# Two heads change places in an attention and feed-forward kernel, and its written order of work is replaced

## The chip, the cores and the metric

The kernel runs on one core of one Trainium2 chip. The metric is the device time of one execution in microseconds (us); the time shown for the kernel before is the median of three runs. A profile is one execution seen by the hardware profiler; its "span" runs from the first to the last instruction of the program and is shorter than the device time.

The engines are named as the profile names them: PE is the matrix engine, PEld its weight loads, DVE the vector engine, ACT the scalar engine, POOL the general-purpose engine, SP the engine that only issues transfers (DMAs). "SPq" is SP's queue of instructions. A transfer that has arrived is said to have landed.

## The reference: what is computed

Four batches, eight heads, 768 positions, 64 numbers a head. Heads 0, 2 and 6 are "retrieval" heads: plain causal attention. The other five are "streaming" heads: a position sees the first four positions (the sink) and the last 64 (the window). The heads' outputs side by side are x (3072 rows of 512), and a feed-forward layer follows:

```python
scores = q @ k.T / sqrt(64)                    # per batch and head
keep   = causal if retrieval[h] else causal & (sink | last 64)
a      = softmax(where(keep, scores, -1e9))
x      = concat over heads (a @ v)             # 3072 x 512, float32
h      = x @ w_in                              # w_in 512 x 2048
out    = (h * sigmoid(beta * h)) @ w_out       # w_out 2048 x 512
```

## The kernel before, in words

**Units.** The work is cut into eight units: batch b and half u of the positions (384 queries each), n = 2b + u. Each unit goes through the same stages. Its q, k and v are loaded in float32 and cast to bfloat16; q and k are turned (units 0 to 2: by PE transposes of tile `c`, units 3 to 7: by DMA transposes `QK<-c`, called `turn_block`); PE makes the scores S(n, ...) into two-bank PSUM tiles `sp`; ACT takes the exponential into `es`; DVE multiplies masks in; PE adds up the exponentials (`sums` in units 0 and 1, `sums_d` later); PE multiplies with v (`pv`) into `sp` again; DVE multiplies by the reciprocal sums R (`norm`) into `xT`, four tiles of 128 x 384, each tile two heads of 64 rows. Then come 16 tiles `mm1` (w_in against `xT`, four matmuls into one PSUM bank `b`), for each a tanh on ACT (`swish_a`, output `t`) and a multiply on DVE (`swish_b`, output `gT`), and 48 matmuls `mm2` against w_out, copies (`osb`) and stores.

**The reciprocals' round trip.** In units 2 to 7 the sums go from PSUM to `sc`, by DMA to `rec` (`sums_turn`), through a DVE reciprocal, by DMA to a scratch in DRAM (`spread_w`, `rd<-rec`), and from there by DMA to all 64 rows of every head (`spread_r`, `R<-rd`; in odd units one small `q2f<-rd` more). `norm` needs it.

**Which heads share a tile.** `PAIRS` says which two heads are loaded, turned and scored together: (0, 2), (1, 3), (4, 5), (6, 7). `XT` says which two heads share a tile of `xT`: (1, 0), (2, 3), (4, 5), (6, 7). The rows of w_in must lie in the same order, so the rows of heads 1 and 0 are loaded swapped. `ORDER` and `QUARTERS` say where each head's sums lie; `spread_r` uses as many DMAs as it needs for rows at even distances in that order.

**Loading weights.** w_in and w_out come in four quarters of 1 MB each. A quarter of w_in (`load_w_in`) takes three DMAs, a quarter of w_out one. They land in a ring `wf` of three buffers, which v and the blocks of q and k (`load_block`) use too; POOL casts each in four parts (below: wi0 to wi15 and wo0 to wo15, four per quarter). A new load waits until an earlier buffer has been cast.

**The written order.** Every piece of work is a task, given to `add` with its engine, a price in us, what it needs, what it gives, and which ring buffers it takes. There are 1096. `SEQUENCE` is a list of their numbers and `CHOICE` a letter for each of 97 tasks that may run on one of several engines. `_Plan.run` walks the list and places each task as early as its engine and its needs allow:

```python
for o in (self.ops[i] for i in SEQUENCE):
    ...
    t = max([now[e]] + [done[n][0] - ... for n in needs])
    ...
    end = t + cost
    was, now[e] = now[e], end
    ...
    if dma:
        bus = max(bus, t + (0.5 if dma > 0.2 else cost)) + dma
        end = bus + (1.9 if dma > 0.2 else 3.2)
    order.append((t, i, f, e, t - was))
return [x[2:] for x in sorted(order, key=lambda x: x[:2])]
```

The tasks are emitted in order of their planned times, and every engine keeps that order (`_Ordered`). So on one engine the tasks follow each other as `SEQUENCE` has them, and a task that waits holds up all that follow on its engine. The prices decide only the planned times, not the length of anything on the chip. Line L112, which nearly every row of the profile names, is the helper that emits all instructions; rows are told apart by their tiles.

**Transfers share eight semaphores.** In the trace every DMA from the ninth on waits for the one eight before it to land. SP issues nearly all of them, in order, so a load that waits for a buffer also holds back the ones behind it.

**Start.** SP loads q, and ACT the first four k. PE runs filler matmuls in planned gaps of unit 0. A task `const_table` (an Exp of one column, on ACT) stands early in ACT's order.

Of the kernel before, what the change touches and what calls it, by code (L numbers as in the profile page):

```python
# [16 lines left out]
PAIRS = [(0, 2), (1, 3), (4, 5), (6, 7)]  # L17
XT = [(1, 0), (2, 3), (4, 5), (6, 7)]
# [10 lines left out]
QUARTERS = [[[1, 0], [2, 3], [4, 5], [6, 7]], [[2], [6], [0], [3, 5, 7, 1, 4]]]  # L29
# [3 lines left out]
ORDER = [[1, 0, 2, 3, 4, 5, 6, 7], [2, 6, 0, 3, 5, 7, 1, 4]]  # L33
# [4 lines left out]
    474, 475, 6, 466, 4, 8, 14, 468, 12, 478, 467, 20, 10, 0, 2, 16, 5, 469, 473, 9, 7, 33, 471, 29, 77, 34,  # L38
    31, 13, 89, 32, 15, 30, 37, 477, 18, 50, 38, 39, 51, 11, 79, 40, 85, 1, 56, 43, 52, 3, 490, 35, 25, 41,
    27, 36, 26, 57, 42, 28, 17, 44, 45, 21, 47, 78, 91, 48, 53, 80, 97, 54, 59, 86, 102, 480, 23, 100, 24,  # L40
    101, 58, 103, 60, 49, 116, 19, 46, 117, 118, 55, 61, 22, 120, 62, 463, 121, 485, 479, 492, 119, 122, 73,
    493, 90, 63, 92, 491, 123, 114, 75, 64, 74, 81, 115, 112, 76, 83, 125, 481, 65, 87, 126, 67, 113, 69, 484,
    66, 134, 482, 71, 68, 135, 483, 137, 108, 70, 500, 139, 109, 72, 488, 520, 82, 93, 524, 138, 84, 104, 464,
    140, 127, 489, 95, 465, 528, 521, 494, 105, 522, 529, 486, 532, 536, 495, 136, 525, 487, 530, 106, 142,
    526, 88, 533, 143, 534, 502, 540, 107, 98, 110, 503, 547, 505, 111, 94, 541, 128, 548, 131, 501, 542, 551,
    132, 124, 555, 141, 129, 96, 549, 556, 559, 133, 159, 130, 560, 504, 557, 99, 144, 552, 510, 499, 553,
    155, 145, 497, 537, 498, 538, 157, 156, 496, 146, 515, 507, 563, 158, 509, 561, 570, 508, 564, 160, 147,
    523, 571, 148, 506, 527, 565, 572, 163, 531, 167, 153, 149, 151, 511, 535, 171, 150, 512, 161, 152, 574,
    513, 165, 154, 578, 575, 514, 173, 582, 579, 576, 169, 580, 586, 583, 218, 518, 592, 584, 476, 587, 517,
    596, 588, 516, 470, 597, 519, 539, 593, 598, 162, 543, 546, 594, 168, 222, 550, 172, 554, 174, 170, 184,  # L50
    185, 558, 544, 164, 166, 562, 190, 186, 188, 191, 193, 175, 189, 566, 187, 600, 221, 196, 569, 573, 192,
    601, 577, 194, 581, 567, 219, 181, 602, 198, 220, 604, 199, 197, 182, 224, 608, 201, 200, 585, 609, 195,
    227, 225, 203, 605, 610, 589, 223, 204, 606, 228, 612, 202, 206, 590, 205, 619, 613, 207, 226, 176, 208,
    620, 177, 623, 621, 209, 591, 614, 210, 627, 631, 229, 628, 635, 632, 629, 237, 633, 636, 235, 642, 568,
    624, 637, 239, 646, 238, 650, 211, 647, 625, 240, 212, 178, 472, 269, 595, 651, 648, 241, 599, 652, 242,
    654, 179, 643, 249, 655, 603, 236, 252, 644, 213, 658, 250, 253, 607, 656, 659, 244, 660, 611, 247, 271,
    615, 245, 618, 622, 243, 251, 616, 254, 248, 273, 626, 180, 255, 630, 257, 183, 634, 246, 256, 638, 258,
    272, 641, 639, 259, 270, 617, 645, 260, 649, 261, 214, 216, 231, 215, 280, 653, 232, 657, 217, 275, 661,
    664, 662, 274, 278, 668, 665, 276, 672, 669, 666, 277, 676, 262, 673, 230, 233, 670, 674, 677, 279, 678,
    680, 684, 681, 691, 682, 263, 685, 695, 326, 692, 686, 699, 693, 696, 703, 700, 697, 707, 663, 701, 714,  # L60
    704, 708, 718, 289, 705, 709, 715, 722, 726, 716, 264, 723, 234, 667, 727, 290, 281, 671, 724, 293, 282,
    728, 675, 719, 283, 291, 730, 720, 679, 731, 292, 315, 284, 295, 732, 683, 296, 687, 298, 690, 694, 688,
    300, 297, 698, 319, 303, 294, 327, 301, 302, 702, 304, 328, 706, 265, 299, 329, 267, 266, 689, 305, 330,
    545, 268, 710, 306, 713, 717, 307, 721, 370, 725, 317, 736, 729, 737, 321, 740, 738, 316, 711, 733, 324,
    741, 744, 318, 734, 748, 320, 742, 745, 752, 322, 749, 746, 323, 756, 308, 753, 750, 763, 754, 325, 757,
    767, 764, 758, 771, 640, 765, 768, 775, 309, 772, 366, 769, 779, 773, 776, 786, 777, 790, 787, 286, 780,
    788, 334, 332, 285, 739, 335, 287, 794, 336, 781, 743, 795, 310, 337, 791, 796, 747, 338, 792, 798, 339,
    369, 802, 799, 346, 367, 803, 800, 751, 349, 373, 368, 804, 755, 347, 376, 759, 762, 288, 760, 341, 372,
    766, 344, 333, 375, 770, 340, 342, 371, 774, 343, 374, 351, 350, 345, 778, 354, 348, 377, 782, 352, 785,
    311, 353, 355, 313, 312, 356, 789, 357, 314, 793, 358, 386, 797, 331, 387, 735, 801, 390, 712, 412, 808,  # L70
    388, 812, 809, 378, 392, 813, 810, 805, 395, 379, 814, 816, 391, 783, 359, 380, 820, 806, 817, 360, 824,
    416, 821, 818, 828, 822, 825, 835, 393, 826, 839, 396, 829, 836, 397, 830, 843, 389, 837, 840, 847, 361,
    844, 841, 851, 394, 848, 845, 415, 858, 849, 862, 852, 413, 859, 866, 853, 414, 860, 870, 863, 417, 864,
    400, 811, 419, 871, 815, 398, 418, 872, 422, 819, 867, 823, 868, 421, 399, 874, 401, 381, 827, 875, 420,
    402, 876, 362, 403, 404, 364, 363, 761, 831, 834, 423, 365, 838, 842, 429, 846, 880, 832, 850, 405, 881,
    431, 406, 882, 884, 807, 432, 382, 383, 888, 885, 892, 889, 886, 384, 854, 424, 890, 893, 857, 433, 861,
    426, 833, 855, 865, 407, 894, 869, 385, 896, 900, 425, 897, 434, 898, 907, 436, 911, 901, 784, 908, 873,
    902, 856, 877, 909, 912, 915, 878, 913, 919, 430, 916, 879, 427, 923, 920, 917, 930, 924, 921, 934, 435,
    925, 938, 931, 942, 932, 939, 408, 943, 940, 410, 409, 935, 883, 887, 411, 946, 944, 443, 936, 947, 891,
    895, 446, 447, 948, 952, 444, 953, 438, 954, 899, 441, 903, 439, 956, 442, 445, 906, 957, 448, 437, 958,  # L80
    910, 449, 914, 451, 450, 440, 918, 904, 960, 452, 453, 922, 454, 961, 926, 455, 964, 962, 968, 965, 905,
    929, 969, 933, 966, 937, 970, 428, 941, 945, 927, 949, 456, 972, 928, 950, 457, 979, 973, 983, 980, 974,
    987, 981, 984, 991, 988, 985, 995, 989, 992, 1002, 996, 993, 458, 1006, 997, 1003, 1010, 1007, 1004, 1014,
    1008, 1018, 1015, 955, 1011, 1016, 1012, 1019, 951, 1020, 959, 963, 967, 971, 975, 978, 976, 982, 977,
    986, 990, 994, 998, 1001, 999, 1005, 459, 460, 1000, 461, 1009, 462, 1013, 1017, 1021, 1024, 1022, 1028,
    1025, 1023, 1032, 1029, 1026, 1036, 1030, 1033, 1040, 1037, 1034, 1044, 1038, 1041, 1051, 1045, 1042,
    1055, 1046, 1052, 1059, 1056, 1053, 1063, 1057, 1060, 1067, 1064, 1061, 1073, 1065, 1068, 1076, 1069,
    1079, 1077, 1027, 1080, 1078, 1031, 1081, 1074, 1082, 1075, 1085, 1083, 1035, 1086, 1084, 1039, 1087,
    1043, 1047, 1048, 1050, 1054, 1049, 1058, 1062, 1066, 1070, 1088, 1071, 1089, 1072, 1092, 1090, 1091,
    1093, 1094, 1095,  # L90
]
CHOICE = (
    "aaddagaggdgdadadadaadddaddaaddgaagggdaaadaadaaaddaaaddaggdgdgaggadggdgdaadaadaaadaadadadddadddaaa"
# [95 lines left out]
def kernel(  # L189
# [282 lines left out]
    def load_w_in(s):  # L472
        f = stg.tile([128, 2048], F32, name="wf", bufs=RINGS["wf"]).rearrange("p (a n) -> p a n", a=NP)

        def rows(r, n, tiles):
            return bass.AP(moe_w_in.tensor, moe_w_in.offset + r * d_ff + s * 2 * FS,
                           [[d_ff, n], [128 * d_ff, tiles], [1, 2 * FS]])
        sp.dma_start(out=f[:, 1:4, :], in_=rows(128, 128, 3))
        sp.dma_start(out=f[0:D, 0:1, :], in_=rows(D, D, 1))
        sp.dma_start(out=f[D:128, 0:1, :], in_=rows(0, D, 1))  # L480
        wst["i", s] = f
# [483 lines left out]
    def attention(n, early):  # L965
# [3 lines left out]
        for pi in range(NP if n < TD else 0):  # L969
            for nm in ("q2", "k2"):  # L970
                e = "act" if n == 0 and nm == "k2" else "sp"
                add(e, 0.47, lambda pi=pi, nm=nm, e=e: load_qk(x, pi, nm, ENG[e]), dma=0.63,
                    gives=[("f", n, pi, nm)], take=[(nm + "f", (n, pi), 1)])
                e = ("pool", "dve", "act") if early else ("pool",)
                add(e, [{"dve": 0.3, "pool": 0.47, "act": 0.41}[i] for i in e],
# [265 lines left out]
```

## Time and profile before

| what | value |
|---|---|
| device time, median of 3 runs | 242.45 us (241.02 to 242.52) |
| span of the profiled execution | 238.9 us |
| around the span, against the median | 3.55 us |
| PE busy | 224.3 us, 94% of the span |
| DVE, ACT, POOL busy | 153.9, 141.9, 90.8 us |
| mean granted clock of PE | 0.979 |
| moved by DMA | 43.14 MB |

How to read it: an engine's busy time is the union of its instructions. PE's matmuls overlap, so its busy time includes some slack that no row shows. "40 slices" cut the span in pieces of 6.0 us; a digit is a share in tenths. In a list of waits, "A <- B" means that A's engine stood idle until B had finished. The profiled execution's device time is not given; the span plus the 3.55 us stands for it.

### The profile page before, as it was taken

The page shows a single profiled execution, that of the slowest core. Times are in us where ns is not written, and L with a number is a line of the kernel's source. Part 1 is how long each engine was busy: PE and PEld are TensorE (multiplying, and loading weights), DVE is VectorE, ACT ScalarE, POOL GpSimd, SP SyncE. Part 2 cuts the span into 40 slices and gives each one's busy share as a digit, 9 for nine tenths or more (in the row PEclk, how much of TensorE's full clock was granted, in tenths as well). Part 3 has the DMA queues.
Part 4 walks back from the last instruction along what each step waited for, and adds up shares of the span by engine and source line. Part 5 has one row for each costly group of instructions (what it writes and reads, how often), then busy time and mean ns, then how long its engine had stood idle before and what let it go on. Part 6 is the DMA issues. An engine that isn't in the chain of part 4 may idle for free.

```text
span 238.9 us, 6057 instructions
## 1 busy us (share of the span) xinstructions
PE 224.3 (94%) x2359; PEld 128.6 (54%) x2385; DVE 153.9 (64%) x354; ACT 141.9 (59%) x238; POOL 90.8 (38%) x199
## 2 busy tenths in 40 slices
PE   8678996999999999999999999999999999999994
PEld 8535555555555456546544545564465555466553
DVE  4539869783968838865686548787475477157620
ACT  3858785456889518761679569707677437107611
POOL 7204759587632845696536173403600000000000
PEclk9956999999999999999999999999999999999999
DMA  6999699999989979999998999789910026211012
GB/s 197 273 307 321 205 258 354 300 314 211 175 196 240 211 162 189 214 230 223 225 231 179 169 230 231 149 178 216 219 71 3 0 92 150 80 44 47 0 44 88
DMA packets 92108, 43.14 MB, mean 181 GB/s; under 512 B 75936, under 2 KB 84848, under 8 KB 92080
## 3 DMA queue, kind: packets, MB, share of 16 engines
q1 hardware_dynamic: 90992, 41.98, 76.0%
q10 hardware_dynamic: 1088, 0.79, 1.1%
q8 instruction: 18, 0.29, 0.5%
q14 instruction: 10, 0.08, 0.1%
HBM read 32.38 MB, written 6.37 MB: 162 GB/s over the span
## 4 chain that ended last, share of the span: by engine, by line
PE 70%; DMA 9%; DVE 8%; SPq 4%; POOL 3%; ACT 3%; issue 2%; POOLq 0%
PE b L112 60%; PE sp L112 10%; SPq L112 4%; DMA QK<-c 3%; DMA wf<-in_v_dram 2%; POOL c L112 2%; DMA wf<-in_k_dram 2%; DMA q2f<-in_q_dram 2%; DVE es L112 2%; DVE gT L112 1%; ACT t L112 1%; DVE vs L112 1%; DVE QK L112 1%; ACT es L112 1%; DVE KP L112 1%
## 5 line engine op out<-in xcount | busy, mean ns | idle before, releaser
L112 ACT ACTIVATE t<-b,beta_h 128x384 f32<-128x384 f32 x128 | 72.4, 582 | 40.3 <-PE b L112 29.2
L112 DVE SCALAR_TENSOR_TENSOR gT<-t,b 128x384 bf16<-128x384 f32 x128 | 68.9, 551 | 37.1 <-ACT t L112 33.2
L112 PE MATMUL b<-xT,w_in 128*128 128x384 bf16 x512 | 90.3, 326 | 1.4 <-POOL w_in L112 0.9
L112 PE MATMUL b<-w_out,gT 128*128 128x512 bf16 (+1 forms) x374 | 87.1, 370 | 2.7 <-issue 1.8
L112 PEld LDWEIGHTS <-w_in 128*128 128x128 bf16 x512 | 49.0, 98 | 38.7 <-issue 2.6
L112 PEld LDWEIGHTS <-gT 128*128 128x128 bf16 x400 | 36.9, 98 | 38.7 <-issue 2.4
L112 ACT ACTIVATE es<-sp 128x768 bf16<-128x768 f32 (+3 forms) x64 | 49.1, 806 | 11.1 <-PE sp L112 10.7
L112 POOL CAST c<-wf 128x256 bf16<-128x256 f32 x60 | 23.2, 432 | 21.2 <-DMA wf<-in_q_dram 13.7
L112 PE MATMUL sp<-QK 64*64 64x64 bf16 (+6 forms) x402 | 19.9, 242 | 4.0 <-DVE QK L112 1.5
L112 ACT ACTIVATE osb<-b 128x512 f32<-128x512 f32 (+1 forms) x14 | 8.0, 568 | 23.9 <-PE b L112 16.9
L112 PEld LDWEIGHTS <-QK 64*64 64x64 bf16 (+1 forms) x402 | 10.4, 107 | 15.2 <-issue 12.1
L112 POOL COPY KP<-QK 128x64 bf16<-128x64 bf16 (+4 forms) x36 | 10.2, 332 | 21.6 <-DMA QK<-c 21.6
L112 POOL CAST w_in<-wf 128x512 bf16<-128x512 f32 x16 | 10.7, 699 | 15.2 <-DMA wf<-in_moe_w_in_dram 15.2
L112 POOL CAST vb<-wf 128x512 bf16<-128x512 f32 x18 | 12.2, 696 | 11.2 <-DMA wf<-in_v_dram 11.1
L112 DVE TENSOR_TENSOR es<-es,mask_c 128x256 bf16<-128x256 bf16 (+2 forms) x32 | 12.1, 394 | 4.2 <-ACT es L112 4.0
L112 DVE TENSOR_TENSOR es<-es,mask_s 128x800 bf16<-128x800 bf16 (+5 forms) x24 | 12.9, 551 | 2.7 <-ACT es L112 2.7
L112 DVE TENSOR_TENSOR xT<-sp,R 128x768 bf16<-128x768 f32 (+3 forms) x18 | 11.6, 687 | 4.0 <-PE sp L112 3.9
L112 DVE TENSOR_SCALAR osb<-b 128x512 f32<-128x512 f32 x11 | 7.5, 681 | 9.9 <-PE b L112 7.7
L112 PE MATMUL sp<-es,vb 128*64 128x64 bf16 (+3 forms) x243 | 13.8, 237 | 0.0
L112 POOL COPY vs<-vb 64x1536 bf16<-64x1536 bf16 (+2 forms) x9 | 12.2, 1361 | 2.5 <-issue 2.1
L112 PEld LDWEIGHTS <-vb 128*64 128x64 bf16 x243 | 11.8, 111 | 0.3
L112 POOL CAST w_out<-wf 128x512 bf16<-128x512 f32 x16 | 10.1, 667 | 2.2 <-DMA wf<-in_moe_w_out_dram 2.1
(91 smaller groups left out, 169.8 us busy)
## 6 DMA issues: line engine op xcount, KB each, us to landing
out_dram<-osb SPq DMA_DIRECT2D x23, 256.0 KB
wf<-in_v_dram SPq DMA_DIRECT2D x18, 256.0 KB
wf<-in_moe_w_out_dram SPq DMA_DIRECT2D x4, 1024.0 KB
wf<-in_q_dram SPq DMA_DIRECT2D x15, 256.0 KB
wf<-in_k_dram SPq DMA_DIRECT2D x15, 256.0 KB
R<-rd SPq DMA_DIRECT2D x9, 384.0 KB
wf<-in_moe_w_in_dram SPq DMA_DIRECT2D x4, 768.0 KB
q2f<-in_q_dram SPq DMA_DIRECT2D x12, 192.0 KB
```

Source lines behind the costliest of these rows:

```text
L112: ins = f(*a, **k)
```

## The change

One: `XT` becomes `PAIRS`, so tile 0 of `xT` holds heads 0 and 2, and tile 1 heads 1 and 3. `QUARTERS` and `ORDER` of even units follow: 0, 3, 1, 2 in place of 1, 0, 2, 3.

Two: `load_w_in` still issues three DMAs for a quarter: before, 768 KB on 128 partitions and twice 128 KB on 64; now 512 KB and twice 256 KB, all on 128 partitions.

Three: `spread_r`, whose code is the same, now needs three DMAs in place of two in units 2, 4 and 6, and four in place of three in 3, 5 and 7 (the small one not counted), because the heads' places are less even.

Four: prices of some tasks change, and `SEQUENCE` and `CHOICE` are new throughout.

```diff
-XT = [(1, 0), (2, 3), (4, 5), (6, 7)]
+XT = PAIRS
-QUARTERS = [[[1, 0], [2, 3], [4, 5], [6, 7]], [[2], [6], [0], [3, 5, 7, 1, 4]]]
+QUARTERS = [[[0, 3], [1, 2], [4, 5], [6, 7]], [[2], [6], [0], [3, 5, 7, 1, 4]]]
-ORDER = [[1, 0, 2, 3, 4, 5, 6, 7], [2, 6, 0, 3, 5, 7, 1, 4]]
+ORDER = [[0, 3, 1, 2, 4, 5, 6, 7], [2, 6, 0, 3, 5, 7, 1, 4]]
 SEQUENCE = [
-    474, 475, 6, 466, 4, 8, 14, 468, 12, 478, 467, 20, 10, 0, 2, 16, 5, 469, 473, 9, 7, 33, 471, 29, 77, 34,
+    474, 12, 14, 0, 8, 2, 475, 466, 479, 10, 6, 463, 469, 13, 478, 37, 15, 39, 4, 468, 473, 471, 477, 1, 25,
...
 def load_w_in(s):
-        sp.dma_start(out=f[:, 1:4, :], in_=rows(128, 128, 3))
-        sp.dma_start(out=f[0:D, 0:1, :], in_=rows(D, D, 1))
-        sp.dma_start(out=f[D:128, 0:1, :], in_=rows(0, D, 1))
+        sp.dma_start(out=f[:, 2:4, :], in_=bass.AP(moe_w_in.tensor, at + 4 * D * d_ff, [[d_ff, 128], [2 * D * d_ff, 2], cols]))
+        for t in range(2):
+            sp.dma_start(out=f[:, t, :], in_=bass.AP(moe_w_in.tensor, at + t * D * d_ff, [[2 * D * d_ff, 2], [d_ff, D], cols]))
...
-            add("sp", [1.33, 2.65][u], lambda: spread_r(x), ... dma=[6.2, 6.0][u],
+            add("sp", [2.0, 2.65][u], lambda: spread_r(x), ... dma=[3.8, 3.9][u],
...
-            add("sp", 1.3 if w == "i" else 0.65, ..., dma=3.5, ...)
+            add("sp", 1.6 if w == "i" else 0.5, ..., dma=3.1 if w == "i" else 2.9, ...)
```

The other prices that change: loads of q and k 0.63 to 0.65, blocks 3.5 to 3.65, v 3.5 to 3.6, `sums_turn` in odd units 1.5 to 1.7, `const_mask_new` 0.75 to 1.4.

What the new order says at the start, as the numbers of the tasks decode. Each engine's list, before and after:

```
SP before:  q of pairs 1 2 3, v2, q pair 0, v0 | unit 1: q0 q3, v1 (unit 0), k0 q2, wi4-7 (3 DMAs), k3, v2 (unit 1), wi0-3 (3), beta, wo0-3, q1 k1 k2, wi8-11, v0 v1, wo4-7, ...
SP after:   q of pairs 3 0 2, beta, q pair 1, v0 | unit 1: q0 q1 k0 q2 q3, v1 (unit 0), k2, v2 (unit 0), k3, wi0-3 (3 DMAs), k1, wi4-7 (3), wo0-3, wi8-11, v2 v1 v0, wo4-7, ...
ACT before: four loads of k, const_table among them; one cast; then copies and exponentials
ACT after:  four loads of k; two casts; then copies and exponentials; const_table is the 19th from the end
```

Ahead of `pv` of unit 1 PE has 10 tiles of `mm1` before and 12 after; ahead of the first `mm1` it has 14 groups of scores before and 16 after. The work on PE in total is the same list of tasks.

## Prediction

> **What bounds the kernel now.** I read the page first, then busy time in stretches of 10 us, then PE's waits, then the chain of waits and the timelines of the start.
>
> ```profile
> span 238.9 us, 6057 instructions
> ...
> PE 224.3 (94%) x2359; PEld 128.6 (54%) x2385; DVE 153.9 (64%) x354; ACT 141.9 (59%) x238; POOL 90.8 (38%) x199
> ...
> PEclk9956999999999999999999999999999999999999
> DMA  6999699999989979999998999789910026211012
> ```
>
> PE is the bound, at full clock but for the slices around 12 to 24 us; the transfers are about as full until some 170 us. The stretches show where PE has room:
>
> ```profile
> 0.00:10.00 10.00, 7.71 (x99) 6.99 (x99) 4.25 (x27) 5.50 (x11) 4.71 (x28) 1.00 0.89 227
> 10.00:20.00 10.00, 6.85 (x63) 3.64 (x63) 5.85 (x18) 6.58 (x11) 1.61 (x3) 0.61 1.13 307
> 20.00:30.00 10.00, 9.35 (x140) 6.19 (x139) 9.20 (x20) 8.18 (x13) 6.96 (x11) 0.88 0.80 249
> 30.00:40.00 10.00, 7.92 (x113) 4.61 (x115) 7.97 (x16) 7.57 (x14) 6.88 (x12) 1.00 1.09 297
> 40.00:50.00 10.00, 9.95 (x122) 6.13 (x113) 7.95 (x17) 4.61 (x8) 6.66 (x12) 1.00 1.01 321
> ```
>
> PE's busy time is the first figure after each length. It lacks 8.2 us before 40 us and hardly anything afterwards. From 40 us on PE waits for others only this much:
>
> ```profile
> PE b L112 <- issue: 1.8, 11, 0.2
> PE sp L112 <- DMA QK<-c: 0.5, 1, 0.5
> PE b L112 <- DVE gT L112: 0.2, 1, 0.2
> ```
>
> So a new order can win only in the first 40 us, and can lose anywhere. The start ends where PE last waits for data. That is `pv` of unit 1, which needs `vs`, a DVE copy:
>
> ```profile
> 39.08 1.51 DVE L112 COPY vs<-vb 64x1536 bf16<-64x1536 bf16 x2
> ```
>
> PE begins that `pv` at 40.66 and is full from there. One later place is as tight: the scores of unit 5 start right behind a chain of loads, casts and DMA transposes.
>
> ```profile
> 108.63 5.09 DMA wf<-in_k_dram
> ...
> 113.77 3.53 POOL c L112 x10
> ...
> 119.42 3.81 DMA QK<-c
> 123.27 0.50 PE sp L112 x4
> ```
>
> **Heads in pairs: PE and DVE.** In `pv` the first tile now pairs two retrieval heads and the second two streaming heads; before, one of each stood side by side. In the trace of `pv` of unit 2 the two halves of PE run side by side either way. The two mixed tiles took 0.573 us (85.411 to 85.984). Heads 4 and 5, both streaming, took 0.22 us for seven matmuls a side. One side's retrieval head took 0.187 + 0.109 + 0.056 = 0.35 us for its 384, 256 and 128 columns. New: 0.35 + 0.22 = 0.57 us. I take 0; bounds -0.05 and +0.1 us a unit. Sums, masks and `norm` keep counts and shapes.
>
> **Weights on 128 partitions.** In the quarter that landed around 19 us the 768 KB took 2.68 us (from the landing before it, by the trace's semaphore events), the halves 0.56 and 0.33. That is 0.89 us for 256 KB on 64 partitions, and 2.68 / 3 = 0.89 on 128. Three DMAs stay three, each about 0.5 us of SP. I take 0. Upper bound: as dear per MB as v, 1.15 us for 256 KB, so +1.0 us a quarter. Lower: as cheap as w_out, whose 1 MB landed 2.32 to 2.67 us after the landing before, so -0.9 to -1.2 us a quarter. Casts on POOL and the PE work ahead cover either, as the next part shows; with that cover gone the first quarter alone would move PE.
>
> **The start in the new order.** DMAs land one behind another: 0.65 us for q or k, 1.15 for v, 3.5 for w_in, 2.4 for w_out. Before, they landed with holes: q of pair 3 of unit 1 came 2.09 us after the last instead of 0.65, and with the waits for `wf` buffers there are about 4.7 us of holes up to 50 us. In the new order v2 no longer stands ahead of unit 0's last pair, and no load meets a buffer still in use. So I get unit 0's q and k by 8.4 us (before 9.43), the first two w_in quarters by 24.0 (before 24.9), the third by 30.0 (33.7), the last w_out by 45 (50.1). The first four casts of w_in end near 22.7 (before 27.3). Weights then wait for nobody in the first 40 us; before, one wait was 0.92 us.
>
> What remains is ACT and DVE. With casts of 0.45, copies 0.45, exponentials 0.75 and 0.2 us from engine to engine, ACT runs nearly without a hole from the first exponential at about 9.3 us to its last one before the first `swish_a`, which starts near 28.0; before it was 30.03. On DVE the spread constants (`sel`, 0.75) and a copy of `R` (0.96) leave the chain to the first `norm`. Then come masks, ten `swish_b` at 0.5, two casts of v and `vs` at 1.5, which ends near 38.8. So `pv` of unit 1 starts near 39.0 instead of 40.66, with 12 tiles of `mm1` done instead of 10. A tile is 0.65 us (eight matmuls in 1.47, less the last one's tail). Gain: 1.66 + 2 x 0.65 = 3.0 us. A hand count over some forty links may be off by 0.05 a link: bounds -5.0 (all holes filled) and +1.
>
> **The table load speaks against it.** `const_table` now stands near the end. Before, its load ran while ACT waited for data:
>
> ```profile
> 1.87 1.28 ACT L112 ACT_TABLE_LOAD   x1 [1.87 <-issue]
> ...
> 3.17 0.20 ACT L112 ACTIVATE warm<-warm 128x1 f32<-128x1 f32 x1
> 5.07 0.51 ACT L112 CAST c<-q2f 128x384 bf16<-128x384 f32 x1 [1.70 <-DMA q2f<-in_q_dram]
> ```
>
> It stands right ahead of the first ACTIVATE. In the new order the first is unit 0's first exponential; casts and copies are other operations in the trace. Behind it queue all of ACT's exponentials and copies, for which PE's two `sp` buffers wait. Cost between 0 (ahead of the casts again) and 1.28; I take +1.28, nearest to the row. The dummy itself, 0.20 us near the end, is hidden by ACT's waits for PE (29.2 us in all).
>
> The Trainium skill ("ScalarE: Activation LUTs", What ACT_TABLE_LOAD costs) gives about 1283 ns for the load plus about 1380 ns of drain, some 2.66 us a switch. The row agrees on 1.28 and shows no drain: ACTIVATE starts 0.02 us after the load. By the page the sum below would be 1.4 us worse, 242.2.
>
> **Reciprocals.** One more issue in `spread_r`, 0.6 us of SP. The bytes are the same, and the data takes longer (1.94 us per 384 KB) than an issue, so I take 0; without that cover R lands 0.65 later. The cushion is thin: R landed 2.4, 2.2, 1.9, 2.5, 3.9 and 6.8 us before `norm` in units 2 to 7. In the new order PE has less work between `sums_d` and `pv`: by 1.5, 1.8, 2.6, 1.2, 2.5 and 3.9 us, counted in tiles at 0.65, `mm2` at 0.216, `sums_d` 0.6 to 0.9 and `pv` 1.2 to 1.9. With the 0.65 off, units 3 and 4 are short by 0.3 and 1.35. But on SP their R has less ahead of it: in unit 3 two loads of v (7.0 us) give way to a block (3.6) and three small loads (0.6); in unit 4 a block and six small loads (4.8) to a load of v (3.5). Left: 0.05 in unit 4. I take +0.3 in all; bounds 0 and +1.65. Late next would be `norm`, then `mm1`, with every `swish_b` queued behind `norm` on DVE.
>
> **Scores of unit 5.** PE reaches them three tiles (1.95 us) earlier by the order, and 1.7 earlier by the start: at 122.8 - 3.65 = 119.1. Their transposes landed at 123.2. In the new order unit 5's v (3.5) moves behind them, nine small loads (1.6) and one store fewer (0.7) change places, and unit 3's transposes come 2.7 earlier: 123.2 - 2.6 - 2.7 = 117.9. The wait of 0.48 goes: I take -0.3; bounds -0.48 and +4.1 (no gain on that chain).
>
> **Sum.** Span 238.9 plus 3.55 around it is the median, 242.45. -3.0 (start) + 1.28 (table) + 0.3 (reciprocals) - 0.3 (unit 5) + 0 (weights, `pv`, `spread_r`'s issue) = -1.7. Time 240.8 us.
>
> **Rivals.** A change of 1% (2.4 us, bounds 240.0 and 244.9) is about what a measurement of this kernel can tell from no change.
>
> *Free table load, whole start.* The load sits ahead of the casts, where ACT waits for its first q: 242.45 - 3.0 + 0.3 - 0.3 = 239.5; a point lower if more of the holes is won. For it: ACT is idle until 4 us. Against: the row's place right ahead of ACTIVATE.
>
> *The chain of transfers sets the pace.* Between 50 and 160 us the transfers are as full as PE. If the chain to unit 5's transposes wins nothing, PE stands at the scores of unit 5 until 123.3 with three tiles fewer done: the start's gain is gone and 1.95 us are added. Unit 4's reciprocals, on the same queue, add their 1.35: 242.45 + 1.95 + 1.35 = 245.7, slower. It decides from the point where the transposes land later than 119.1 + 1.7 + 1.95 = 122.8. For it: the old wait stands there, and cushions shrink everywhere. Against: the loads that moved away.
>
> *128 partitions do more than the row says.* w_in at w_out's rate saves 0.9 us a quarter: three quarters matter by 40 us, 2.7 us of transfers. A third of it reaching PE gives 239.9. Against: equal rates in the row.
>
> **How the numbers follow.** Forecast 240.8: 0.42 (own range 239.3 to 242.5); free table load: 0.26; chain of transfers: 0.24; weights: 0.08. Faster by over 1%: 0.10 of the first case, 0.23 of the second, 0.05 of the last, 0.38. Slower by over 1%: 0.02 of the first, 0.24 of the third, 0.26. Within 1%: 0.36. The range, 237.0 to 246.0, takes in more of the holes filled (-5.0 of the start instead of -3.0, table free) and the chain's 245.7.
>
> **What would show it.** Right: `pv` of unit 1 begins near 39 to 40.3 with 12 tiles done; the table load stands ahead of an `es` row near 9 to 10.5 us; w_in quarters take 3.5 us; PE waits under 1 us after 42 us; unit 5's scores start near 119. Wrong: PE rows waiting for `QK<-c` or for `xT` by over 2 us in all after 42 us, a first `swish_a` after 30 us, or ACT waiting long for stores (`osb`), which I left out.

## The result, and the profile after

The kernel after takes **280.56 us** (median of 4 runs, 279.36 to 280.91), the kernel before 242.03 us (4 runs, 241.02 to 242.52). The ratio is 1.1595, with a 95% interval of 1.1554 to 1.1635. Executions of one kernel fall into a fast and a slower state, and ratios compare fast ones alone, so a median over all runs can lie above what its ratio says. The forecast was 240.8 us with a range of 237.0 to 246.0: wrong by 40 us and in its sign.

The page of the kernel after, the lines that answer to those shown of before:

```profile
span 279.2 us, 6011 instructions
...
PE 229.1 (82%) x2331; PEld 128.1 (46%) x2357; DVE 151.9 (54%) x353; ACT 139.5 (50%) x233; POOL 89.2 (32%) x205
...
PEclk9996595758859999999999999999999999999999
DMA  7954361377857997999979999899993101430212
```

PE's work has grown little (224.3 to 229.1 us, with a lower clock in the fourth to the twelfth slice). The span has grown by 40.3 us, so PE stands still. The DMA line shows where: from 14 to 56 us (the third to the eighth slice, of 7 us each) the transfers are 0.1 to 0.6 busy, and 0.5 around 80 us; before, they were 0.9 nearly throughout. The stretches of 10 us (PE busy first after the length; the last three figures are PE's clock, the DMA share and GB/s):

```profile
10.00:20.00 10.00, 8.19 (x150) 4.91 (x148) 9.26 (x26) 9.90 (x18) 3.42 (x8) 1.00 0.79 201
20.00:30.00 10.00, 2.47 (x53) 1.41 (x47) 3.00 (x7) 3.26 (x5) 0.70 (x2) 0.68 0.35 112
...
40.00:50.00 10.00, 4.58 (x15) 2.22 (x16) 0.72 (x2) 1.75 (x3) 3.46 (x6) 0.54 0.15 54
```

Up to 20 us the new order runs ahead of the old one: PE has 8.19 us of work at a clock of 1.00, where it had 6.85 at 0.61. Then PE starves while the transfers are nearly empty: 0.15 of 16 engines is 2.4 engines. What PE waits for, over the whole span (us in total, times, longest):

```profile
PE b L112 <- POOL w_in L112: 27.4, 3, 10.1
PE b L112 <- POOL c L112: 8.0, 1, 8.0
PE sp L112 <- DMA QK<-c: 3.2, 2, 1.8
```

Casts of `w_in` are late three times. The fourth wait, for `c`, is a cast of k that stands behind a cast of `w_in` on POOL. These four waits are 35.4 us of the 40.3. The chain of waits says what the casts wait for (start, length, what):

```profile
37.90 19.93 DMA wf<-in_moe_w_in_dram
...
62.96 18.00 DMA wf<-in_moe_w_in_dram
```

These two loads of 256 KB take 18 to 20 us from issue to landing; right behind each stand the casts of `w_in` and then PE's `mm1`. By the trace's semaphore events the eight DMAs that bring tiles 0 and 1 of `w_in` landed 4.81 to 6.27 us after the landing before them (first quarter: 18.32, then 23.58 and 29.16 us). The plain 512 KB load of the first quarter took 1.73 us.

### The profile page after: what moved, and what is told of

Its sections match the earlier page's. It is cut to its first block, busy times and chain, and to the rows that moved or that the text cites. A ratio compares the mean times of both kernels' runs of the same rounds, so it can differ in the third digit from the quotient of the medians.

```text
span 279.2 us, 6011 instructions
## 1 busy us (share of the span) xinstructions
PE 229.1 (82%) x2331; PEld 128.1 (46%) x2357; DVE 151.9 (54%) x353; ACT 139.5 (50%) x233; POOL 89.2 (32%) x205
## 4 chain that ended last, share of the span: by engine, by line
PE 47%; DMA 24%; SPq 15%; DVE 5%; POOL 4%; issue 2%; ACT 2%; DVEq 0%; POOLq 0%; ACTq 0%
PE b L112 42%; SPq L112 15%; DMA wf<-in_moe_w_in_dram 14%; PE sp L112 5%; DMA out_dram<-osb 2%; DMA vf<-in_v_dram 2%; DMA q2f<-rd 2%; DMA q2f<-in_q_dram 2%; DVE gT L112 2%; ACT t L112 1%; DMA QK<-c 1%; DVE vs L112 1%; DMA wf<-in_k_dram 1%; POOL c L112 1%; POOL w_in L112 1%
## 5 line engine op out<-in xcount | busy, mean ns | idle before, releaser
L112 PE MATMUL b<-xT,w_in 128*128 128x384 bf16 x512 | 96.6, 343 | 28.5 <-POOL w_in L112 27.4
L112 PE MATMUL b<-w_out,gT 128*128 128x512 bf16 (+1 forms) x374 | 86.2, 371 | 2.2 <-issue 1.4
L112 PEld LDWEIGHTS <-w_in 128*128 128x128 bf16 x512 | 50.3, 102 | 69.5 <-POOL w_in L112 29.5
L112 POOL CAST c<-wf 128x256 bf16<-128x256 f32 x60 | 24.1, 442 | 34.2 <-DMA wf<-in_k_dram 17.8
L112 POOL CAST w_in<-wf 128x512 bf16<-128x512 f32 x16 | 9.3, 622 | 45.7 <-DMA wf<-in_moe_w_in_dram 24.5
L112 POOL COPY KP<-QK 128x64 bf16<-128x64 bf16 (+5 forms) x41 | 11.3, 321 | 27.0 <-PE b L112 11.8
L112 DVE TENSOR_TENSOR xT<-sp,R 128x768 bf16<-128x768 f32 (+3 forms) x18 | 11.7, 687 | 10.4 <-PE sp L112 9.4
L112 DVE TENSOR_TENSOR es<-es,mask_c 128x256 bf16<-128x256 bf16 (+2 forms) x32 | 10.8, 344 | 8.1 <-ACT es L112 7.7
L112 PE MATMUL b<-ident,c 128*128 128x128 bf16 x72 | 7.4, 236 | 8.9 <-POOL c L112 8.0
L112 DVE TENSOR_TENSOR es<-es,mask_s 128x800 bf16<-128x800 bf16 (+5 forms) x24 | 12.8, 538 | 1.1 <-ACT es L112 1.1
L112 DVE TENSOR_SCALAR osb<-b 128x512 f32<-128x512 f32 (+1 forms) x10 | 6.6, 660 | 11.9 <-PE b L112 8.9
L112 POOL COPY vs<-vb 64x1536 bf16<-64x1536 bf16 (+2 forms) x10 | 12.4, 1252 | 0.4
L112 PEld LDWEIGHTS <-vb 128*64 128x64 bf16 x243 | 10.6, 111 | 3.7 <-issue 2.0
```

The costliest lines, as they stand in the source:

```text
L112: ins = f(*a, **k)
```

## The experiments

The theory: the loads of tiles 0 and 1 are slow because their source lists two heads outermost, `[[2 * D * d_ff, 2], [d_ff, D], cols]`, and only two DMA engines then take part. (An access pattern is a list of [step, count] pairs; the first pair is the outermost, and its count is called the outermost size below.) The rival: the new order is at fault, and slow transfers are its result. Parts of the change were taken alone and the load was given other forms. Below, "ratio" is to runs of the kernel before on the same chip, with its 95% interval.

**The load's form, in both orders.** `new_order_64` is the kernel after with these two loads instead:

```diff
-        for t in range(2):
-            sp.dma_start(out=f[:, t, :], in_=bass.AP(..., at + t * D * d_ff, [[2 * D * d_ff, 2], [d_ff, D], cols]))
+        for i in range(2):
+            sp.dma_start(out=f[i * D:(i + 1) * D, 0:2, :],
+                         in_=bass.AP(..., at + i * 2 * D * d_ff, [[d_ff, D], [D * d_ff, 2], cols]))
```

> The kernel after, with one edit: tiles 0 and 1 of w_in come in two DMAs of 64 partitions (heads 0 and 1, then heads 2 and 3), whose source lists 64 rows outermost, in place of two DMAs of 128 partitions whose source lists 2 heads outermost. Same bytes, still three DMAs a quarter. Theory (the form of the two loads costs it all, about 4.6 us more for each of eight DMAs): each 256 KB lands about 0.9 us behind the one before it instead of 5.5, the four holes of PE (7.9, 9.3, 7.9 and 10.1 us) go, and the time is 237 to 242 us. Rival (the new order itself puts the casts of w_in too early or too late, and the transfers are slow because the queues are crowded): the holes stay in part and the time stays above 260 us.

Measured: 250.87 us, ratio 1.0309 (1.0243 to 1.0374). The long waits shrink (PE waits 4.4 us for `w_in`, not 27.4), so some 30 us of the loss are the form of the load. But the time isn't at 237 to 242, and 0.9 us a load isn't reached either: the two took 0.8 to 1.3 us each.

`old_order_128` takes the kernel before, with its order and prices, and puts in the paired heads and the slow load:

```diff
-XT = [(1, 0), (2, 3), (4, 5), (6, 7)]
+XT = PAIRS
...
-        sp.dma_start(out=f[:, 1:4, :], in_=rows(128, 128, 3))
-        sp.dma_start(out=f[0:D, 0:1, :], in_=rows(D, D, 1))
-        sp.dma_start(out=f[D:128, 0:1, :], in_=rows(0, D, 1))
+        # the three DMAs of the kernel after
```

> The order and the prices of before, with the heads of each unit renamed to pairs and with the two loads of w_in as in the kernel after (2 heads outermost in the source). Theory (the form of the loads costs it all): each 256 KB lands some 5.5 us behind the one before it here too, and the time is 270 to 285 us. Rival (the new order is at fault): 241 to 246 us.

Measured: 276.35 us, ratio 1.1462 (1.1408 to 1.1517). The old order suffers nearly as much, so the rival that blames the order for the long waits falls. `old_order_64` is the same with the loads of `new_order_64`:

> The order and the prices of before, heads in pairs, with tiles 0 and 1 of w_in in two DMAs of 64 partitions each (64 rows outermost in the source). This leaves the pairing of the heads as the only change to before. Theory (pairing costs nothing on PE, DVE or ACT, as forecast): 241.5 to 243.5 us. Rival (pairs of one kind make pv or the masks longer): above 244 us.

Measured: 246.28 us, ratio 1.017 (1.0112 to 1.0229). That is the rival's range: something beside the slow loads costs about 4 us here, and the loads on 64 partitions or the pairs may be it.

**The loads by themselves.** `dma_alone` (a new, small kernel: `for groups in (128, 2, 4, 8, 16, 64, ...): dma_start(f, source with that outermost size)`, each waiting for the last):

> Leaves out the whole computation: only 256 KB loads of w_in rows onto 128 partitions, one after another, each waiting for a small DVE copy of the one before; the source's outermost dimension has 128, 2, 4, 8, 16, 64, and then 2, 4, 8, 16, 64, 128 entries, then come four 128 KB loads on 64 partitions and stores. Theory (the outermost size sets how many of the 16 DMA engines share a transfer): the time beyond a fixed part is about 5.5 us for 2, 2.8 for 4, 1.4 for 8, and 0.7 to 0.9 for 16, 64 and 128 alike. Rival (the slow loads were slow through crowding by other queues, or through the order of rows in memory): all sizes take the same within 20%.

Its chain of waits (start, length, what), the loads with 128, 2, 4 and 16 outermost of the first of the two passes:

```profile
0.73 3.09 DMA f<-in_moe_w_in_dram
...
4.10 7.10 DMA f<-in_moe_w_in_dram
...
11.40 4.82 DMA f<-in_moe_w_in_dram
...
20.47 3.07 DMA f<-in_moe_w_in_dram
```

The same 256 KB, the same 128 partitions, nothing else in flight: 3.1 us with 16, 64 or 128 outermost, 3.8 with 8, 4.8 with 4, 7.1 with 2. The second pass (2, 4, 8, 16, 64, 128) gave 7.39, 5.13, 4.00, 3.15, 3.11 and 3.13. With k for the outermost size, at most 16, a fixed 2.5 us plus 0.6 us times 16 / k fits them: 7.3, 4.9, 3.7 and 3.1 us for k of 2, 4, 8 and 16. The rival (crowding, or the order of rows: all alike) falls. The trace shows the engines more directly. Each load with 2 outermost raises its semaphore in three steps, the first of them early and two at the landing; a load with 4 does so in five, with 8 in nine, and with 16, 64 or 128 in sixteen. The slow loads of the kernel after have three steps too. The Trainium skill has the rule ("DMA: Bandwidth & Descriptors", section "Why a DMA increments its semaphore by 16 and not by 1"): the engines that share a transfer are the largest number up to 16 that divides the outermost dimension, counted without those of size 1, of both access patterns. The runs agree (two, four, eight and sixteen steps at the landing), and the prediction had not looked at the source's side.

`dma_rates` asks what each form costs when the queue is full (eight groups of 2 MB, `for g in groups: g(); wait for all of g`):

> Leaves out the whole computation: eight groups of loads of w_in, 2 MB each, the loads of a group issued one behind another without a wait and a wait for the whole group between groups. Groups: 256 KB on 128 partitions; 512 KB (two tiles) on 128 partitions; 256 KB (two tiles) on 64 partitions; 128 KB on 64 partitions; 256 KB with 2 heads outermost; then quarters as in the kernel before (768 + 2 x 128 KB), as in new_order_64 (512 + 2 x 256 KB on 64 partitions) and with 512 + 4 x 128 KB. Theory (each engine that takes part moves at one rate, so only the outermost size of 2 is slow): about 0.65 to 0.9 us per 256 KB in every group but the fifth, 4.5 to 5.5 us each there; the three forms of a quarter within 10% of one another. Rival (two tiles on 64 partitions are slow by themselves, which would explain that new_order_64 is 3% behind before): that group takes 1.1 to 1.3 us per 256 KB, and its quarter is at least 20% slower than that of the kernel before.

| form, back to back | us per 256 KB, by landings |
|---|---|
| 256 KB on 128 partitions | 1.35 |
| 512 KB, two tiles, 128 partitions | 0.93 |
| 256 KB, two tiles, 64 partitions | 1.13 |
| 128 KB, 64 partitions | 1.50 (SP issues one each 0.64 us) |
| 256 KB, 2 heads outermost | 5.13 |

The second quarter of each mixed group took 3.27 us as in the kernel before, 3.83 as in `new_order_64`, and 3.27 with 512 + 4 x 128 KB. So the rival is half right: two tiles on 64 partitions are slow, and that quarter is 17% dearer. The theory holds for the form with 2 outermost: 5.13 less 0.82 (a quarter of 3.27) is 4.3 us a load, 34.5 us for eight. From 57 to 90 us, where only such loads are in flight, the DMA share is 0.13, about two engines of 16. The slow form also holds up the engine that issues. Of the chain in that group:

```profile
71.56 5.00 SPq L56
76.60 18.47 DMA f<-in_moe_w_in_dram
```

SP took 0.6 us for each of the first two of these eight issues, 2.94 to 7.16 us for the next four, and 5.00 us for each of the last two: about one issue for each load that landed. In the kernel after, SP's issues behind the slow loads took as long (4.86, 4.55 and 5.19 us), and everything on SP's queue stood behind.

**The load as four halves.** `new_order_halves` and `old_order_halves` load tiles 0 and 1 as the kernel before loads its one mixed tile:

```diff
+        for t in range(2):
+            for i in range(2):
+                sp.dma_start(out=f[i * D:(i + 1) * D, t, :],
+                             in_=bass.AP(..., at + (2 * i + t) * D * d_ff, [[d_ff, D], cols]))
```

> The kernel after with tiles 0 and 1 of w_in in four DMAs of 128 KB on 64 partitions each, the form that the kernel before has for its one mixed tile. Two more issues a quarter on SP, some 0.6 us each. Theory (two tiles on 64 partitions were the trouble of new_order_64): 239 to 244 us. Rival (the order is at fault, or any load on 64 partitions): 246 to 252 us as in new_order_64.

> The order and prices of before, heads in pairs, the same four DMAs of 128 KB on 64 partitions. Theory (heads in pairs cost nothing by themselves): 241 to 243 us, 0.995 to 1.01 of before. Rival (heads in pairs cost PE or DVE time): 244 us or more, as in old_order_64.

Measured: 245.78 us, ratio 1.0167 (1.0113 to 1.0221) in the new order, between the two expectations; 245.01 us, ratio 1.0168 (1.012 to 1.0216) in the old one, in the rival's range. Against the 1.1595 of the kernel after, the form of the load alone is worth 0.143 x 242 = 34.5 us in the new order; against the 1.1462 of `old_order_128`, 0.129 x 242 = 31.3 us in the old one. `dma_rates` gives 34.5 us for eight loads; that the first figure is the same is partly luck, since not all of a transfer's delay need reach PE. The rest, 4 us, does not come from sources with two heads outermost.

**The order alone.** `new_order_old_heads` has the new order and prices, and heads and loads of before:

```diff
-XT = PAIRS
+XT = [(1, 0), (2, 3), (4, 5), (6, 7)]
...
+        sp.dma_start(out=f[:, 1:4, :], in_=rows(128, 128, 3))   # and the two halves, as before
```

> The new order and prices alone: heads and loads of w_in as in the kernel before. Theory (the order brings what the forecast said, and new_order_64 lost it in its loads of w_in): 238 to 241 us, in this comparison 0.985 to 1.0 of before. Rival (the order itself is worse, because the scores of later units wait for the transfers and casts that were moved): 244 to 250 us, 1.01 to 1.035 of before, with PE waiting over 2 us for QK<-c after 42 us.

Measured: 246.05 us, ratio 1.0215 (1.0165 to 1.0264). The order by itself loses 5 us: the rival's time, though PE waits 1.8 us for `QK<-c`, not over 2. Two of its stretches:

```profile
20.00:30.00 10.00, 8.33 (x101) 4.65 (x97) 6.90 (x17) 6.75 (x12) 6.36 (x11) 1.00 1.07 312
...
40.00:50.00 10.00, 6.15 (x27) 2.46 (x26) 5.48 (x15) 1.91 (x4) 5.39 (x11) 0.93 1.05 317
```

`pv` of unit 1 begins at 37.27 us (before: 40.66) with 12 tiles of `mm1` done (before: 10). But from 40 to 50 us PE has 6.15 us of work where it had 9.95, at a DMA share of 1.05. PE's waits name the weights:

```profile
PE b L112 <- POOL w_in L112: 3.9, 3, 1.9
PE b L112 <- POOL w_out L112: 2.0, 3, 1.1
PE sp L112 <- DMA QK<-c: 1.8, 2, 1.1
```

Up to 50.7 us PE is idle for 12.8 us (before: 8.2), from there to its last matmul for 3.8 (before: 3.3).

**Fewer bytes in the start.** If the full transfers are what the new order runs into, halving the bytes of `w_in` must free it. In both kernels the casts write tiles 0 and 1 a second time as 2 and 3:

```diff
-        cast(eng, w_in_sb[...][:, :, c], wst["i", s][:, :, i * 128:(i + 1) * 128])
+        cast(eng, w_in_sb[...][:, :, c].rearrange("p (r t) n -> p r t n", r=2),
+             wst["i", s][:, None, 0:2, i * 128:(i + 1) * 128].to_broadcast([128, 2, 2, 128]))
```

> The kernel before with half the bytes of w_in: tiles 0 and 1 are loaded (256 KB and two of 128 KB), and the casts write them a second time as tiles 2 and 3, so the output is that of other weights; all other work is the same. Theory (transfers are full from 10 to 50 us and set the pace of the start): weights come about 1.7 us earlier a quarter, PE's waits for w_in (0.9 us) go, 239.5 to 241 us, 0.99 to 1.0 of before. Rival (transfers have room): no change beyond 0.3%.

> The new order with heads and loads as before, as new_order_old_heads (1.0215 of before), and with half the bytes of w_in as in before_half_w_in; the output is that of other weights. Theory (the new order gains its 3.4 us at pv of unit 1 and loses them, and more, to weights that the full transfers cannot bring sooner): PE's waits for w_in and w_out in the first 50 us (5.9 us in new_order_old_heads) fall below 2 us, and the time falls by 3 to 5 us to 241 to 243 us; what stays of the loss is the later waits for QK<-c, vs and osb, about 3 us. Rival (the order loses elsewhere): still 1.015 of before or more, 245 us.

Measured: 240.89 us, ratio 0.9949 (0.9914 to 0.9983) for the old order; 240.76 us, ratio 0.9943 (0.991 to 0.9976) for the new one. (The old order's interval still touches the 0.3% of its rival.) PE's waits for `w_in` and `w_out` in the first 50 us fall from 5.9 to 1.0 us in the new order. The new order gains 0.027 of 242, 6.6 us, from the missing bytes, the old one 1.2 us. PE's idle time up to 50.7 us falls from 12.8 to 6.1 us in the new order, where the old one with half the bytes has 9.2: the 3 us that the forecast promised appear once the transfers have room. They don't become time, because PE, which comes earlier now, waits more later. In `order_half_w_in`:

```profile
PE sp L112 <- DMA QK<-c: 3.0, 3, 1.8
PE b L112 <- DVE osb L112: 1.9, 1, 1.9
```

From 50.7 us to its last matmul PE is idle for 8.5 us there, against 3.2 in `before_half_w_in` and 3.8 in `new_order_old_heads`; the waits for transposes and stores are most of it. In all it is idle for 14.6 us against 12.4, and the two times are alike because it was also busy for 2.0 us less (221.8 against 223.8 us).

**Five loads in the old order.** Does `old_order_halves` lose its 1.7% through two DMAs more a quarter? `before_five_loads` changes nothing else:

```diff
-        sp.dma_start(out=f[:, 1:4, :], in_=rows(128, 128, 3))
+        sp.dma_start(out=f[:, 2:4, :], in_=rows(256, 128, 2))
+        for i in range(2):
+            sp.dma_start(out=f[i * D:(i + 1) * D, 1:2, :], in_=rows(128 + i * D, D, 1))
```

> The kernel before, heads and order untouched, with tile 1 of w_in taken out of the 768 KB load and brought in two more DMAs of 128 KB on 64 partitions: five DMAs a quarter, as in old_order_halves, where PE got the third quarter's weights 2.4 us later than in the kernel before. Theory (old_order_halves lost its 1.7% through its loads, each quarter 4.7 us instead of 3.6 in the transfers and two issues more on SP): 244 to 246 us, 1.01 to 1.02 of before. Rival (the pairing of heads costs it): 241 to 242.5 us, 0.995 to 1.005.

Measured: 242.9 us, ratio 1.0053 (1.0018 to 1.0088), between the two expectations. The loads explain 0.5% of the 1.7%. The other 1.1% comes with the paired heads, but only in the old order: in the new one the paired heads with halves (1.0167) are no slower than the old heads (1.0215). That points to an order made for other heads rather than to a cost of the pairs.

The traces narrow it. `pv` takes 1.28 to 1.29 us in units 2, 4 and 6 and 1.99 us in 3, 5 and 7, in the kernel before and in `old_order_halves` alike, so the pairs cost nothing there. `pv` of unit 1 begins at 44.10 us in `old_order_halves` (before: 40.66) and the last matmul ends 3.7 us later than before, so nearly all of that execution's loss lies in the start, ahead of the first `spread_r`, at 79 us. There the third quarter's weights landed at 36.08 us (before: 33.68). Behind the wait for them, `mm1` and then the spreading of the sums ran slowly. Before, and in `old_order_halves`:

```profile
36.80 1.47 PE L112 MATMUL b<-xT,w_in 128*128 128x384 bf16 x8 [0.92 <-POOL w_in L112]
...
39.27 1.47 PE L112 MATMUL b<-es,esel 128*32 128x128 bf16 x60
```

```profile
39.62 2.10 PE L112 MATMUL b<-xT,w_in 128*128 128x384 bf16 x8 [2.52 <-POOL w_in L112]
...
41.76 2.41 PE L112 MATMUL b<-es,esel 128*32 128x128 bf16 x60
```

The granted clock was 0.67 in the first of these two rows (39.6 to 41.7 us) and 0.50 at the beginning of the second (41.7 to 43); together they lose 1.6 us. That is one execution. Whether this makes up the 1.1%, and why the weights were that late for PE with these heads, stays open.

## Why the prediction was wrong, and where it was right

**The step that failed: "Weights on 128 partitions".** It priced the two new loads by their bytes and by the partitions they fill, took 0, and set +1.0 us a quarter as the upper bound. By `dma_rates` each cost 4.3 us more than it would at the rate of before, 8.6 a quarter, 34.5 in all; the kernels themselves lost 34.5 us by it in the new order and 31.3 in the old. The row it leaned on (768 KB in 2.68 us, "0.89 on 128") is of DMAs whose source lists 128 rows outermost; the halves list 64. The change's source lists 2, and no `w_in` load of before has that form. The number of partitions says nothing on that; the prediction treated a form that its row didn't show as if it were shown. The rival on this part ("128 partitions do more than the row says") had the sign wrong too. The part says that "casts on POOL and the PE work ahead cover either", and that with that cover gone the first quarter would move PE: cover for a microsecond a quarter met a delay of 8.6.

**The start: the mechanism was right, the limit wasn't seen.** Forecast: `pv` of unit 1 at 39.0 with 12 tiles done. With the loads and heads of before it began at 37.27 with 12 tiles done. The failed term is "about 4.7 us of holes up to 50 us" in the transfers. From 10 to 50 us the kernel before moves 11.7 MB by its stretches (307, 249, 297 and 321 GB/s), `new_order_old_heads` 11.6 MB (274, 312, 261, 317), and the DMA share of before over these 40 us, in the prediction's own rows, has a mean of 1.01: there was next to nothing to fill. A late landing is no empty pipe, and a price taken from the spacing of two landings (0.65, 3.5 us) isn't kept when loads crowd: the first two quarters of `w_in` took 4.4 and 4.3 us there. They landed by 25.84 (forecast 24.0), the third by 32.18 (30.0), and the last `w_out` at 49.95 (45). "Weights then wait for nobody in the first 40 us" failed with it.

**The scores of unit 5** were to lose their wait of 0.48. In `new_order_old_heads` they start at 124.99 after a wait of 0.73, and a group at 101.57 waits 1.07. The forecast took -0.3 and gave the rival "the chain of transfers sets the pace" 245.7 us. The order alone measured 246.05: near that number, but by luck, less through the rival's place (1.8 us of waits for `QK<-c`) than through the weights up to 50 us.

**The table load** was put at +1.28 us, right ahead of the first ACTIVATE. It stands ahead of a cast:

```profile
2.89 1.28 ACT L112 ACT_TABLE_LOAD   x1 [2.89 <-issue]
4.19 0.51 ACT L112 CAST c<-q2f 128x384 bf16<-128x384 f32 x1
```

The cast's q landed at 4.03 us, so it cost at most 0.16 us. What the prediction drew from "casts and copies are other operations in the trace", that the load would wait for the first ACTIVATE (8.77 us here), was wrong; the rival "free table load" had this part right.

**Reciprocals and `pv`.** The +0.3 for the cushions didn't show: in the kernel after and in `new_order_64`, PE never waits for `xT` after 50 us; in the kernel after everything was late, so its cushions weren't tried there. `pv` of paired heads costs nothing, as forecast: the same 1.28 to 1.29 and 1.99 us in `old_order_halves` as before.

**The base.** "Span 238.9 plus 3.55 around it" is wrong by its second part: in `new_order_64`, a run of 247.71 us has a span of 246.0, so 1.7 us lie around it and the profiled run of before was faster than the median. This changes the forecast by less than 2 us.

## What to carry to other kernels

Price a DMA by its access patterns, not by its bytes and partitions: read the outermost size on both sides, and where a change brings a form that no row of the trace has, say that its price is unknown, and take the price with only a few engines at work as the upper bound. Before you count holes between landings as room, add up the bytes moved in that stretch by the old kernel: if the share is about 1 there, a better order only moves the wait from one operand to the next.

## What the runs showed of the hardware that was not expected

A DMA on few engines also stops its issuer: with a few of them under way, issues on SP took 2.94 to 7.16 us instead of about 0.6, so that every later load on that queue is late too. Back to back, 256 KB on 128 partitions took 1.35 us a load and 512 KB in two tiles 0.93 us per 256 KB; that is one group, the first of its run, and in the two runs with half of `w_in` four of eight such loads landed 0.62 to 0.76 us behind the landing before, so it is no rule. And PE can pay twice for a wait: behind the 2.52 us wait of `old_order_halves`, eight `mm1` matmuls took 2.10 us instead of 1.47, at a granted clock of 0.67. Not every wait does it: behind one of 1.93 us in `new_order_old_heads`, twelve took 2.12 us, at 1.00.
